# Decays kept on the chip, one transfer for r and the values, in a chunked recurrence with a mixture of experts behind it

## The chip, the cores and the metric

The kernel runs on one core of one Trainium2 chip. A core has TensorE (PE; PEld is its weight load), VectorE (DVE), ScalarE (ACT), GpSimd (POOL) and SyncE (SP), which here does nothing but issue transfers to the DMA engines. The metric is device time of one execution in microseconds (us).

## The reference: a recurrence, then a mixture of experts

For 4 sequences, 8 heads, 768 tokens and 40 dimensions a head, a 40 x 40 state is carried from token to token:

```python
for t in range(S):
    y[:, :, t] = np.einsum('bhd,bhde->bhe', rt, state)
    Sa = np.einsum('bhde,bhe->bhd', state, at)
    state_decay = state * wt[:, :, None, :] - np.einsum('bhd,bhe->bhde', Sa, bt)
    state = state_decay + np.einsum('bhd,bhe->bhde', vt, kt)
```

The 3072 x 320 outputs go through 8 experts of width 1024 (two products with a ReLU between). Each token's 8 outputs are weighted with a matrix P, made from a gate's logits by eight rounds of row and column normalisation over all tokens, and added up.

## The kernel before, in words

The sequence is cut into 12 chunks of 64 tokens. A unit of work is one chunk of one sequence, its 8 heads as 4 pairs: 48 units, numbered 4 x chunk + sequence. Each unit has three stages.

*Preparation* (`prep`). SP loads one tile of inputs (inp: decays, k, b, a). DVE makes the decays' running products with two scans (q, L124, and g, L134). POOL or DVE scales k and b (kb, L147) and a (ab, L153 and L154), PE forms the products ll (L159) and transposes kb (kt, L167), DVE masks ll into sx (L169), ACT copies the rest. What the recurrence needs later is kept in one of NSX sets (sx, bb, cc), used in turn: unit n + NSX writes where unit n lay. The running products g themselves are not in a set: they are stored to memory outside the chip (gd, L138) and loaded again (gl, L278) when the unit's output is scaled.

*Inverse*. Two chunks together (8 units) need triangular inverses. The factors are stored (ld), loaded in another layout (lu, L380), inverted in about 40 DVE instructions (L184 to L207), stored (ud, nd, L371 and L372) and loaded again by `tload` as operands for PE (lg, td and tt, L243 to L252); `tmat` makes the last blocks (gp and op, L261 and L266).

*Recurrence* (`recur`), five steps a unit, the four sequences interleaved: av (L289) from the values and the state (vz) and r (rb); f (L290); xc (L297); x and c copies on ACT; pu (L308) with the inverse; pm (L310); c (L315); ws (L317) on DVE; then POOL makes y = ws x decays (L321) and the next state z (L330), which PE transposes (zt) and ACT copies into the next vz.

A list of events with due times gives all this an order in the program, and a planner of the compiler, with a timing model of its own, sets each engine's final order. Every engine works through its instructions strictly in that order, SP too: a transfer that must wait holds up all transfers behind it on SP.

The mixture of experts follows in the same program. Its tiles take the place of the tiles of the attention stage, and its first weights are loaded and cast while the last recurrences run.

Of the kernel before, what the change touches and what calls it, by code (L numbers as in the profile page):

```python
# [11 lines left out]
F32 = mybir.dt.float32  # L12
# [6 lines left out]
C = 64  # L19
NCH = S // C  # L20
# [9 lines left out]
def attention(ctx, tc, d, xd, ps, pq, pt, gs, lg):  # L30
# [5 lines left out]
    io = ctx.enter_context(tc.tile_pool(name="a_io", bufs=1))  # L36
# [12 lines left out]
    sx_b, bb_b, cc_b = ([None] * NSX for _ in range(3))  # L49
    raws = {}  # L50
    for n in range(NCH * NB - NSX, NCH * NB):
        i, pool = n % NSX, sets[n - NCH * NB + NSX]
        if i in IN_SETS or i in KB_SETS:
            raw = pool.tile([128, 1252], F32, name=f"st{i}")
            raws[i] = raw
            sx_b[i] = raw[0:R2, 0:832].rearrange("r (p h x) -> r p h x", h=2, x=104)
            bb_b[i] = raw[:, 832:1248].rearrange("r (p x) -> r p x", x=104)
            cc_b[i] = raw[0:R2, 1248:1252]
            continue
        sx_b[i] = pool.tile([R2, NP, 2, 104], F32, name=f"sx{i}")  # L60
# [26 lines left out]
    def clear():  # L87
# [3 lines left out]
        for t in vz_b + rb_b + c1_b + lg_b:  # L91
            nc.vector.memset(t, 0.0)
# [13 lines left out]
    state = {"sx": 0, "ab": 0, "g1": 0, "vz": 0, "c1": 0, "t1": 0, "tt": 0, "rb": 0, "y": 0}  # L106
# [8 lines left out]
    def prep(c, b, ld):  # L115
# [15 lines left out]
        bb, cc = bb_b[i], cc_b[i]  # L131
        ge = pin.tile([RL, NP, 65], F32, name="g", bufs=2)
# [4 lines left out]
        gd = dr.tile([RL, 320], F32, name=f"gd{cb}", bufs=1)  # L137
        nc.sync.dma_start(out=gd[:, 0:260], in_=ge.rearrange("r p t -> r (p t)"))  # L138
# [40 lines left out]
        return dict(cc=cc, g=gd, sx=sx, bb=bb)  # L179
# [53 lines left out]
    def tload(c):  # L233
# [6 lines left out]
        u = [[slice(cc * 64 + blk * 32 + h * 16, cc * 64 + blk * 32 + h * 16 + 16) for h in range(2)]  # L240
             for blk in range(2)]
# [3 lines left out]
        for h in range(2):  # L245
            nc.sync.dma_start(out=t1[q[h]], in_=nd[u[0][h]].rearrange("g j s -> j g s"))
# [23 lines left out]
    def recur(c, b):  # L270
        pp = preps[c, b]
        vz, zc = vz_cur[b], zp[b]
        nc.sync.dma_start(out=vz[:, :, 0:64], in_=d["v"][c, b])
        rb = rot("rb", rb_b)
        for h in range(2):
            nc.sync.dma_start(out=rb[h * 64:h * 64 + 48, :, h * 64:h * 64 + 64], in_=d["r"][c, b, h])
        gl = io.tile([RL, NP, 65], F32, name="gl", bufs=2)
        nc.sync.dma_start(out=gl.rearrange("r p t -> r (p t)"), in_=pp["g"][:, 0:260])  # L278
# [9 lines left out]
        for p in range(NP):  # L288
            nc.tensor.matmul(av[:, p], lhsT=vz[0:R2, p], rhs=rb[0:R2, p], start=True, stop=True)  # L289
# [31 lines left out]
        nc.gpsimd.tensor_tensor(out=y[0:R2, :, b % 2], in0=ws[:, :, 0:64], in1=gl[0:R2, :, 0:64], op=ALU.mult)  # L321
# [14 lines left out]
        vz = rot("vz", vz_b)  # L336
        nc.scalar.copy(out=vz[0:40, :, 64:104], in_=zt[:, :, 0:40])
        nc.scalar.copy(out=vz[64:104, :, 64:104], in_=zt[:, :, 64:104])
        zp[b] = z
        vz_cur[b] = vz  # L340
# [20 lines left out]
    vz_cur = [rot("vz", vz_b) for _ in range(NB)]  # L361
# [12 lines left out]
    def load_lu(s, n):  # L374
        ld = invs[s][0]
        for cc in range(n):
            for blk in range(2):
                for h in range(2):
                    u0, r0 = cc * 64 + blk * 32 + h * 16, blk * 32
                    nc.sync.dma_start(  # L380
                        out=lu[u0:u0 + 16],
# [454 lines left out]
```

## Time and profile before

| | us |
|---|---|
| median of 3 runs | 1839.33 (1838.09 to 1847.54) |
| the profiled execution | 1832.94 |
| its span, first to last instruction | 1831.2 |
| DMA busy share, 125 to 375 us | 0.79 |

A row of the page or of an answer names the engine, the line, the operation and the tiles (out<-in), then how often it ran, its busy time in us and the mean ns of one, then the engine's idle time before it and what ended that idle time. A wait row reads: who waited, for whom, total us, number of waits, longest. In rows of issues, SPq is SP's queue, and the ns are those of issuing, not of the transfer's landing.

### The profile page before, as it was taken

To read this page: it belongs to the slowest core of one execution; us is meant where nothing else is said; L and a number is where in the kernel's file an instruction comes from. 1 tells how busy PE (TensorE), PEld (TensorE's weight loads), DVE (VectorE), ACT (ScalarE), POOL (GpSimd) and SP (SyncE) were. 2 spreads that over 40 slices of the span, in tenths; PEclk is the share of its full clock that TensorE was granted. 3 is DMA by queue.
4 is the path that set the end of the run, shared out by engine and by line. 5 is a ranking of instruction groups with operands and counts; after the bars stand their busy time and mean duration, and the time that the engine had idled before them with its cause. 6 is when DMAs were issued, how large, how long until landed. Compare 5 with 4: busy or idle time off the path is not lost.

```text
span 1831.2 us, 31655 instructions
## 1 busy us (share of the span) xinstructions
PE 1724.3 (94%) x11843; PEld 1696.8 (93%) x11843; DVE 1365.3 (75%) x2356; ACT 856.8 (47%) x1851; POOL 874.0 (48%) x854
## 2 busy tenths in 40 slices
PE   4479988999989999999999999999999999999999
PEld 4368888898978999999999999999999999999999
DVE  7786996973788867777676878977686877767675
ACT  6347767766743533434343434345343343424342
POOL 6545664723462626447291735008182644628160
PEclk8568988999999999999999999999999999999999
DMA  7468777867520101111020112201020111102001
GB/s 193 116 157 185 175 180 174 186 137 172 152 77 20 57 20 57 38 39 57 20 75 20 57 37 61 69 1 60 16 76 20 57 38 38 57 20 75 15 24 44
DMA packets 211759, 140.47 MB, mean 77 GB/s; under 512 B 162965, under 2 KB 193813, under 8 KB 211605
## 3 DMA queue, kind: packets, MB, share of 16 engines
q1 hardware_dynamic: 207925, 132.70, 27.9%
q10 hardware_dynamic: 3680, 5.74, 1.2%
q8 instruction: 94, 1.54, 0.3%
q14 instruction: 60, 0.49, 0.1%
HBM read 110.78 MB, written 27.61 MB: 76 GB/s over the span
## 4 chain that ended last, share of the span: by engine, by line
PE 75%; DVE 7%; DMA 4%; issue 4%; POOL 3%; ACT 2%; SPq 2%; POOLq 0%; ACTq 0%; DVEq 0%
PE op L647 36%; PE p L582 33%; DMA inp<-in_inp_dram 1%; PE xc L297 1%; PE av L289 1%; PE pu L308 1%; DVE pr L193 1%; DVE hl L606 1%; DVE q L124 1%; PE c L315 1%; DMA ld<-lt 1%; PE op L266 1%; DVE sm L600 1%; PE ll L159 1%; POOL ab L154 1%
## 5 line engine op out<-in xcount | busy, mean ns | idle before, releaser
L582 PE MATMUL p<-xch,wh 128*128 128x384 f32 (+1 forms) x1792 | 605.0, 339 | 8.9 <-DVE sm L600 4.3
L603 ACT ACTIVATE hh<-sm 128x384 fp32r<-128x384 f32 x512 | 269.5, 527 | 728.5 <-DVE sm L600 728.4
L647 PE MATMUL op<-wh,hh 128*128 128x320 f32 x1536 | 477.2, 311 | 4.0 <-ACT hh L603 3.8
L647 PE MATMUL op<-wl,hh 128*128 128x320 f32 x1536 | 474.8, 310 | 0.0
L647 PE MATMUL op<-wh,hl 128*128 128x320 f32 x1536 | 468.0, 309 | 0.9 <-DVE hl L606 0.9
L528 POOL TENSOR_TENSOR wl<-ws,wh 128x640 fp32r<-128x640 f32 x60 | 103.1, 1718 | 606.2 <-ACT wh L526 606.1
L606 DVE SCALAR_TENSOR_TENSOR hl<-sm,hh 128x384 fp32r<-128x384 f32 x512 | 373.1, 762 | 2.6 <-ACT hh L603 1.8
L582 PEld LDWEIGHTS p<-xch,wh 128*128 128x128 f32 (+1 forms) x1792 | 337.0, 188 | 13.3 <-DVE sm L600 5.2
L582 PE MATMUL p<-xcl,wh 128*128 128x384 f32 x896 | 302.3, 337 | 0.0
L582 PE MATMUL p<-xch,wl 128*128 128x384 f32 x896 | 301.8, 337 | 0.0
L647 PEld LDWEIGHTS op<-wh,hh 128*128 128x128 f32 x1536 | 290.2, 189 | 4.9 <-ACT hh L603 4.9
L647 PEld LDWEIGHTS op<-wl,hh 128*128 128x128 f32 x1536 | 291.1, 190 | 0.0
L647 PEld LDWEIGHTS op<-wh,hl 128*128 128x128 f32 x1536 | 286.8, 188 | 1.4 <-DVE hl L606 1.2
L600 DVE TENSOR_TENSOR sm<-p,u 128x384 f32<-128x384 f32 x384 | 236.3, 625 | 8.7
L582 PEld LDWEIGHTS p<-xcl,wh 128*128 128x128 f32 x896 | 168.6, 188 | 0.0
L582 PEld LDWEIGHTS p<-xch,wl 128*128 128x128 f32 x896 | 168.5, 188 | 0.0
L600 DVE TENSOR_TENSOR sm<-p,p 128x384 f32<-128x384 f32 x128 | 71.3, 557 | 129.4 <-PE p L582 75.0
L600 DVE TENSOR_TENSOR p<-p,p 128x384 f32<-128x384 f32 x128 | 71.1, 556 | 101.7 <-PE p L582 101.4
L600 DVE TENSOR_TENSOR u<-p,p 128x384 f32<-128x384 f32 x128 | 70.8, 553 | 57.1 <-PE p L582 55.9
L536 POOL TENSOR_TENSOR wl<-ss,wh 128x512 fp32r<-128x512 f32 x60 | 90.3, 1505 | 28.4 <-ACT wh L533 24.2
L159 PE MATMUL ll<-ab,kb 104*128 104x128 f32 x336 | 62.8, 344 | 40.5 <-POOL kb L147 18.5
L159 PEld LDWEIGHTS ll<-ab,kb 104*128 104x128 f32 x336 | 54.2, 244 | 45.3 <-POOL kb L147 24.8
(163 smaller groups left out, 2727.3 us busy)
## 6 DMA issues: line engine op xcount, KB each, us to landing
ws<-in_wts_dram SPq DMA_DIRECT2D x60, 832.0 KB, 4.5
inp<-in_inp_dram SPq DMA_DIRECT2D x42, 451.5 KB, 4.5
gd<-g SPq DMA_DIRECT2D x48, 113.8 KB, 2.6
gl<-gd SPq DMA_DIRECT2D x48, 113.8 KB, 2.8
vz<-in_v_dram SPq DMA_DIRECT2D x48, 112.0 KB, 3.5
xd<-y SPq DMA_DIRECT2D x24, 224.0 KB, 3.5
ld<-lt ACTq DMA_DIRECT2D x40, 128.0 KB, 2.6
rb<-in_r_dram SPq DMA_DIRECT2D x96, 48.0 KB, 3.1
```

Source lines behind the costliest of these rows:

```text
L124: nc.vector.tensor_tensor_scan(out=qr.rearrange("r p t -> r (p t)"), data0=w65[:, 260:0:-1], data1=one65, initial=0.0, op0=ALU.mult, op1=A ...
L154: eng.tensor_tensor(out=ab[64:104, :, 64:128], in0=a_in[64:104], in1=g[64:104], op=ALU.mult)
L159: nc.tensor.matmul(ll[:, p], lhsT=kb[:, p], rhs=ab[:, p], start=True, stop=True)
L193: nc.vector.tensor_tensor(out=prv, in0=a.unsqueeze(2).broadcast_to([nu, n_c, n_r, n_k]), in1=m.unsqueeze(1).broadcast_to([nu, n_c, n_r, n_ ...
L266: nc.tensor.matmul(op[:, p], lhsT=gs[:, p], rhs=t2[:, p], start=True, stop=True)
L528: g.tensor_tensor(out=wl[:, 0:640], in0=raw[:, 256:896], in1=wh[:, 0:640], op=ALU.subtract)
L536: g.tensor_tensor(out=lv[:, 3:7], in0=so[:, :, 0], in1=hv[:, 3:7, 0], op=ALU.subtract)
L582: nc.tensor.matmul(o, lhsT=w_, rhs=x_, start=(j == 0), stop=(j == 3))
L600: eng.tensor_tensor(out=out, in0=x, in1=y, op=ALU.add)
L603: nc.scalar.activation(out=hh[:, f, h], in_=sm[f][:, h], func=AF.Relu)
L606: v.scalar_tensor_tensor(out=hl[:, f, h], in0=sm[f][:, h], scalar=0.0, in1=hh[:, f, h], op0=ALU.max, op1=ALU.subtract)
L647: nc.tensor.matmul(ops[i], lhsT=a[:, h, cs], rhs=w_[:, cw], start=(f == 0 and h == 0 and j == 0), stop=(last and h == 1 and j == 2))
```

## The change

The running products g stay on the chip: each set gets a fourth part (ge), into which the scan writes and from which y is scaled. The store gd and the load gl are gone. A set is larger by that, and there are 19 instead of 23. The values and r, r already with its zero blocks, lie side by side in one array and come in one transfer into a tile rv of 5 buffers, which also holds the transposed state; before, the values came in one transfer and r in two, one for each head of a pair, r into 2 buffers that had been cleared once. In the inverse's layout the two heads of a pair now alternate instead of lying in two blocks, so that one load brings both: lu takes 2 loads a chunk instead of 4, the operands td 2 instead of 4. Three small constant tiles (pmat, ones, ident) move behind the weights' tiles. In the arithmetic nothing changes.

```diff
-    sx_b, bb_b, cc_b = ([None] * NSX for _ in range(3))
+    sx_b, bb_b, cc_b, ge_b = ([None] * NSX for _ in range(4))
...
-            raw = pool.tile([128, 1252], F32, name=f"st{i}")
+            raw = pool.tile([128, 1512], F32, name=f"st{i}")
...
+            ge_b[i] = raw[0:RL, 1252:1512].rearrange("r (p t) -> r p t", t=65)
...
+        ge_b[i] = pool.tile([RL, NP, 65], F32, name=f"ge{i}")
...
-    vz_b = [const.tile([RL, NP, 104], F32, name=f"vz{i}") for i in range(5)]
+    rv_b = [const.tile([RL, NP, 232], F32, name=f"rv{i}") for i in range(5)]
     c1_b = [const.tile([R2, NP, 104], F32, name=f"c1{i}") for i in range(2)]
-    rb_b = [const.tile([RL, NP, 128], F32, name=f"rb{i}") for i in range(NRB)]
...
-        for t in vz_b + rb_b + c1_b + lg_b:
+        for t in [x[:, :, 192:232] for x in rv_b] + c1_b + lg_b:
             nc.vector.memset(t, 0.0)
...
-        bb, cc = bb_b[i], cc_b[i]
-        ge = pin.tile([RL, NP, 65], F32, name="g", bufs=2)
+        bb, cc, ge = bb_b[i], cc_b[i], ge_b[i]
         g = ge[:, :, 0:64]
...
-        gd = dr.tile([RL, 320], F32, name=f"gd{cb}", bufs=1)
-        nc.sync.dma_start(out=gd[:, 0:260], in_=ge.rearrange("r p t -> r (p t)"))
...
-        return dict(cc=cc, g=gd, sx=sx, bb=bb)
+        return dict(cc=cc, g=g, sx=sx, bb=bb)
...
-        u = [[slice(cc * 64 + blk * 32 + h * 16, cc * 64 + blk * 32 + h * 16 + 16) for h in range(2)]
-             for blk in range(2)]
+        un_, nn_ = ([t[cc * 64 + blk * 32:cc * 64 + blk * 32 + 32].rearrange("(g h) j s -> (h j) g s", h=2)
+                     for blk in range(2)] for t in (ud, nd))
...
-        for h in range(2):
-            nc.sync.dma_start(out=t1[q[h]], in_=nd[u[0][h]].rearrange("g j s -> j g s"))
-        for h in range(2):
-            nc.sync.dma_start(out=t2[q[h]], in_=ud[u[1][h]].rearrange("g j s -> j g s"))
+        nc.sync.dma_start(out=t1, in_=nn_[0])
+        nc.sync.dma_start(out=t2, in_=un_[1])
...
-                nc.sync.dma_start(out=tt[r, :, r], in_=ud[u[blk][h]].rearrange("g j s -> j g s"))
+                nc.sync.dma_start(out=tt[r, :, r], in_=un_[blk][h * 32:h * 32 + 32])
...
-        vz, zc = vz_cur[b], zp[b]
-        nc.sync.dma_start(out=vz[:, :, 0:64], in_=d["v"][c, b])
-        rb = rot("rb", rb_b)
-        for h in range(2):
-            nc.sync.dma_start(out=rb[h * 64:h * 64 + 48, :, h * 64:h * 64 + 64], in_=d["r"][c, b, h])
-        gl = io.tile([RL, NP, 65], F32, name="gl", bufs=2)
-        nc.sync.dma_start(out=gl.rearrange("r p t -> r (p t)"), in_=pp["g"][:, 0:260])
+        rv, zc = rv_cur[b], zp[b]
+        nc.sync.dma_start(out=rv[:, :, 0:192], in_=d["rv"][c, b])
...
-            nc.tensor.matmul(av[:, p], lhsT=vz[0:R2, p], rhs=rb[0:R2, p], start=True, stop=True)
+            nc.tensor.matmul(av[:, p], lhsT=rv[0:R2, p, 128:232], rhs=rv[0:R2, p, 0:128], start=True, stop=True)
...
-        nc.gpsimd.tensor_tensor(out=y[0:R2, :, b % 2], in0=ws[:, :, 0:64], in1=gl[0:R2, :, 0:64], op=ALU.mult)
+        nc.gpsimd.tensor_tensor(out=y[0:R2, :, b % 2], in0=ws[:, :, 0:64], in1=pp["g"][0:R2], op=ALU.mult)
...
-        vz = rot("vz", vz_b)
-        nc.scalar.copy(out=vz[0:40, :, 64:104], in_=zt[:, :, 0:40])
-        nc.scalar.copy(out=vz[64:104, :, 64:104], in_=zt[:, :, 64:104])
+        rv = rot("rv", rv_b)
+        nc.scalar.copy(out=rv[0:40, :, 192:232], in_=zt[:, :, 0:40])
+        nc.scalar.copy(out=rv[64:104, :, 192:232], in_=zt[:, :, 64:104])
...
-                for h in range(2):
-                    u0, r0 = cc * 64 + blk * 32 + h * 16, blk * 32
-                    nc.sync.dma_start(
-                        out=lu[u0:u0 + 16],
-                        in_=ld[cc, r0:r0 + 32].rearrange("j b p h s -> (b p) j h s")[:, :, h, r0:r0 + 32])
+                u0, r0 = cc * 64 + blk * 32, blk * 32
+                nc.sync.dma_start(out=lu[u0:u0 + 32],
+                                  in_=ld[cc, r0:r0 + 32].rearrange("j b p h s -> (b p h) j s")[:, :, r0:r0 + 32])
...
-NSX = 23
+NSX = 19
...
-    pmat = one.tile([128, 24, E], F32, name="pmat")
     lg = one.tile([128, 24, E], F32, name="lg")
-    ones = one.tile([128, 128], F32, name="ones")
-    ident = one.tile([128, 128], F32, name="ident")
...
+    two = ctx.enter_context(tc.tile_pool(name="two", bufs=1))
+    pmat = two.tile([128, 24, E], F32, name="pmat")
+    ones = two.tile([128, 128], F32, name="ones")
+    ident = two.tile([128, 128], F32, name="ident")
...
-    rb = np.zeros((NCH, NB, 2, 48, NP, C), np.float32)
-    rb[:, :, :, 0:40] = split(g["r"])
+    rb = np.zeros((NCH, NB, RL, NP, 2 * C), np.float32)
+    x = split(g["r"])
+    rb[:, :, 0:40, :, 0:C], rb[:, :, 64:104, :, C:] = x[:, :, 0], x[:, :, 1]
...
-    arrays = dict(inp=inp, r=rb, v=packed(g["v"]),
-                  vt=vt, wts=wts, gate=gate, cst=cst)
+    arrays = dict(inp=inp, rv=np.concatenate([rb, packed(g["v"])], -1), vt=vt, wts=wts, gate=gate, cst=cst)
```

What the lines don't show is how the planner orders the engines anew. Two places follow, each first before and then with the change; rows are an engine's instructions in the order of its queue (line, operation, out<-in, shape, "x2" for two alike in a row). The first is SP's queue at the end of the second inverse, where operands of chunk 2 are loaded and the input tiles of later preparations with them. Before:

```order
L276 DMA rb_232<-in_r_dram 48x4x64
L371 DMA ud<-un 64x1024 x2
L372 DMA nd<-tn 64x1024 x2
L278 DMA gl<-gd_431 112x260
L324 DMA xd<-y_234 448x1x128
L138 DMA gd_1468<-g 112x260
L118 DMA inp<-in_inp_dram 112x1032
L276 DMA rb_232<-in_r_dram 48x4x64
L118 DMA inp<-in_inp_dram 112x1032
L243 DMA lg<-ld 32x16x32 x2
L246 DMA td<-nd 32x16x32 x2
```

With the change:

```order
L270 DMA f<-in_vt_dram 64x8x40
L268 DMA rv_205<-in_rv_dram 112x4x192
L361 DMA ud<-un 64x1024
L362 DMA nd<-tn 64x1024
L361 DMA ud<-un 64x1024
L362 DMA nd<-tn 64x1024
L314 DMA xd<-y_213 448x1x128
L118 DMA inp<-in_inp_dram 112x1032
L240 DMA lg<-ld 32x16x32 x2
L242 DMA td<-nd 64x16x32
L118 DMA inp<-in_inp_dram 112x1032
L243 DMA td<-ud 64x16x32
```

The gl, gd and rb transfers between the inverse's stores and the loads of inp are gone, the two td<-nd are one; the values' and r's load is the one row rv.

The second place is DVE around the ws of recurrence 3 (the fourth unit), its first row in both. In brackets stands what the instruction waits for: PE, Activation, Pool and DVE are engines, DMAHW a transfer. Before:

```order
L317 TENSOR_TENSOR ws<-c_1450,c_230 104x416 [waits PE_49,Activation_49]
L128 RECIPROCAL g_223<-q 112x4 [waits DVE_49]
L134 SCALAR_TENSOR_TENSOR g<-inp,g_223 112x260 [waits DMAHW5_49,DVE_49]
L310 TENSOR_TENSOR pm<-pu,cst 128x416 [waits PE_49]
L169 TENSOR_TENSOR sx_205<-ll,cst 64x8x64 [waits PE_49]
L290 TENSOR_TENSOR f<-av,cst 104x8x64 [waits PE_49]
L124 SCALAR_TENSOR_TENSOR q<-inp,cst 112x260 [waits DMAHW7_49,Pool_49]
L169 TENSOR_TENSOR sx_208<-ll,cst 64x8x64 [waits PE_49]
L128 RECIPROCAL g_223<-q 112x4 [waits DVE_49]
L134 SCALAR_TENSOR_TENSOR g<-inp,g_223 112x260 [waits DMAHW4_49,DVE_49]
L317 TENSOR_TENSOR ws<-c_1652,c_229 104x416 [waits PE_49,Activation_49]
```

With the change (ge_176 is the decays' place in the set that unit 3 used and that unit 22 takes over):

```order
L307 TENSOR_TENSOR ws<-c_1319,c_211 104x416 [waits PE_49,Activation_49]
L166 TENSOR_TENSOR sx_169<-ll,cst 64x8x64 [waits PE_49]
L133 SCALAR_TENSOR_TENSOR ge_176<-inp,g_204 112x260 [waits Pool_49]
L300 TENSOR_TENSOR pm<-pu,cst 128x416 [waits PE_49]
L280 TENSOR_TENSOR f<-av,cst 104x8x64 [waits PE_49]
L124 SCALAR_TENSOR_TENSOR q<-inp,cst 112x260 [waits DMAHW5_49,Pool_49]
L128 RECIPROCAL g_204<-q 112x4 [waits DVE_49]
L166 TENSOR_TENSOR sx_173<-ll,cst 64x8x64 [waits PE_49]
L307 TENSOR_TENSOR ws<-c_1428,c_210 104x416 [waits PE_49,Activation_49]
L300 TENSOR_TENSOR pm<-pu,cst 128x416 [waits PE_49]
L124 SCALAR_TENSOR_TENSOR q<-inp,cst 112x260 [waits DMAHW2_49,DVE_49,Pool_49]
L133 SCALAR_TENSOR_TENSOR ge_180<-inp,g_204 112x260 [waits Pool_49]
```

The scan of a preparation (L134 before, L133 now) waited for the store of an earlier scan's result; it now waits for POOL, whose y reads the old decays, and it stands two rows behind the ws that y needs. Of the 29 scans of units 19 to 47 all wait for POOL, and from 1 to 6 instructions lie between ws and scan.

More of the change, by code (lines that the diff above doesn't have):

```diff
@@ L35, in attention @@
     const = ctx.enter_context(tc.tile_pool(name="a_const", bufs=1))
-    io = ctx.enter_context(tc.tile_pool(name="a_io", bufs=1))
     wk = ctx.enter_context(tc.tile_pool(name="a_wk", bufs=2))
@@ L104, in first_use @@
                            in_=cst[64:R2, 360:400].unsqueeze(1).broadcast_to([40, 8, 40]))
-    state = {"sx": 0, "ab": 0, "g1": 0, "vz": 0, "c1": 0, "t1": 0, "tt": 0, "rb": 0, "y": 0}
+    state = {"sx": 0, "ab": 0, "g1": 0, "rv": 0, "c1": 0, "t1": 0, "tt": 0, "y": 0}
     def rot(key, lst):
@@ L335, in recur @@
             nc.tensor.transpose(zt[:, p], z[:, p], ident[0:R2, 0:R2])
-        vz = rot("vz", vz_b)
-        nc.scalar.copy(out=vz[0:40, :, 64:104], in_=zt[:, :, 0:40])
-        nc.scalar.copy(out=vz[64:104, :, 64:104], in_=zt[:, :, 64:104])
+        rv = rot("rv", rv_b)
+        nc.scalar.copy(out=rv[0:40, :, 192:232], in_=zt[:, :, 0:40])
+        nc.scalar.copy(out=rv[64:104, :, 192:232], in_=zt[:, :, 64:104])
         zp[b] = z
-        vz_cur[b] = vz
+        rv_cur[b] = rv
     def gate(c, b, y):
@@ L360, in attention @@
     ys = {}
-    vz_cur = [rot("vz", vz_b) for _ in range(NB)]
+    rv_cur = [rot("rv", rv_b) for _ in range(NB)]
     preps, invs, tts = {}, {}, {}
@@ L431 @@
 SKEW = 1.1
-NSX = 23
+NSX = 19
 GL = 3
 NFB = 3
-NRB = 2
 KB_POOL = (1,2,3,4,5,6,7)
@@ L483, in body @@
         attention(actx, tc, d, xd, ps, pq, pt, gs, lg)
-        nc.gpsimd.memset(ones, 1.0)
-        nc.sync.dma_start(out=ident, in_=d["cst"][:, 232:360])
     stg = ctx.enter_context(tc.tile_pool(name="stg", bufs=2))
@@ L490, in body @@
     x1 = ctx.enter_context(tc.tile_pool(name="x1", bufs=1))
+    two = ctx.enter_context(tc.tile_pool(name="two", bufs=1))
+    pmat = two.tile([128, 24, E], F32, name="pmat")
+    ones = two.tile([128, 128], F32, name="ones")
+    ident = two.tile([128, 128], F32, name="ident")
+    nc.gpsimd.memset(ones, 1.0)
+    nc.sync.dma_start(out=ident, in_=d["cst"][:, 232:360])
     po = ctx.enter_context(tc.tile_pool(name="po", bufs=1, space=bass.MemoryType.PSUM))
```

## The prediction

> **What bounds the kernel now.** I read the page first, then the table of stretches, then the chain and the waits of the stretch that the change touches most.
>
> ```profile
> span 1831.2 us, 31655 instructions
> PEclk8568988999999999999999999999999999999999
> 0.00:125.00 125.00, 65.24 (x347) 58.56 (x348) 94.71 (x171) 58.18 (x145) 73.58 (x105) 0.63 0.65 155
> 125.00:375.00 250.00, 225.99 (x2115) 216.83 (x2113) 201.33 (x343) 180.14 (x455) 145.23 (x170) 0.92 0.79 179
> 375.00:505.00 130.00, 124.42 (x1202) 118.78 (x1201) 80.37 (x149) 84.71 (x202) 44.77 (x54) 0.96 0.65 150
> 550.00:1831.00 1281.00, 1272.65 (x7985) 1269.19 (x7984) 950.90 (x1639) 516.24 (x1019) 580.77 (x500) 1.00 0.13 42
> ```
>
> The last four rows are stretches of the span: length, busy time of PE, PEld, DVE, ACT and POOL, granted clock, DMA share, GB/s. From 550 us on, PE is busy 1272.65 of 1281 us at full clock. That is the mixture of experts, which the change leaves alone, so nothing is to be had there. Everything is decided in the first 505 us: a prologue (to 125) in which DVE is the busiest engine, the recurrence with preparations in between (125 to 375), and the recurrence alone (375 to 505), where PE is busy 96%. In the middle stretch PE is busy 226 and DVE 201 of 250 us, neither full, and the clock is 0.92. Something else ends waits there:
>
> ```profile
> by line: issue 17.0%; DMA inp<-in_inp_dram 10.3%; DVE pr L193 4.6%; PE ll L159 4.1%; POOL ab L154 3.5%; DVE q L124 3.4%; DVE gt L196 3.3%; POOL y L321 3.1%; PE av L289 3.1%; DMA lu<-ld 2.9%; PE xc L297 2.6%; POOL z L330 2.5%; PE op L266 2.4
> DVE q L124 <- DMA inp<-in_inp_dram: 16.6, 8, 5.6
> PE av L289 <- DVE ws L317: 6.6, 3, 3.1
> 152.07 1.61 SPq L372 DMA_DIRECT2D nd<-tn  x2
> 153.78 1.29 SPq L278 DMA_DIRECT2D gl<-gd  x1
> 155.12 0.61 SPq L324 DMA_DIRECT2D xd<-y  x1
> 155.83 0.57 SPq L138 DMA_DIRECT2D gd<-g  x1
> 156.45 0.46 SPq L118 DMA_DIRECT2D inp<-in_inp_dram  x1
> 156.96 0.64 SPq L276 DMA_DIRECT2D rb<-in_r_dram  x1
> 157.70 0.54 SPq L118 DMA_DIRECT2D inp<-in_inp_dram  x1
> 162.46 0.70 DVE L124 TENSOR_TENSOR_SCAN q<-inp,cst 112x260 f32<-112x260 f32 x1 [5.08 <-DMA inp<-in_inp_dram]
> ```
>
> The first row is the chain by line within 125 to 375 us. The largest named item is the load of a preparation's inputs: 10.3% of 250 us, 26 us. DVE waits for it 16.6 us in 8 waits. The timeline under it shows one: SyncE (SP) issues back to back from 152 us on, the load that DVE needs comes last, at 157.70, and DVE stands still 5.08 us until 162.46. So SP's issuing is the resource that is short.
>
> **The change, part by part.** SP's issue cost in this stretch, count and min/median/max ns of an issue:
>
> ```profile
> L276 SPq DMA_DIRECT2D rb<-in_r_dram x56: 564/594/1277, 125.9 to 374.1; - x56
> L273 SPq DMA_DIRECT2D vz<-in_v_dram x25: 572/602/1493, 128.4 to 371.8; - x25
> L278 SPq DMA_DIRECT2D gl<-gd x27: 303/430/1358, 131.0 to 368.4; - x27
> L138 SPq DMA_DIRECT2D gd<-g x29: 304/430/1346, 124.8 to 367.3; - x29
> L380 SPq DMA_DIRECT2D lu<-ld x29: 303/484/1532, 144.6 to 374.8; - x29
> L246 SPq DMA_DIRECT2D td<-nd x12: 420/598/1057, 160.0 to 353.3; - x12
> SPq L278 <- POOL y L321: 12.5, 9, 2.7
> SPq L138 <- DVE g L134: 10.6, 12, 1.7
> ```
>
> *Issues removed.* By medians: r 56 x 0.594 = 33.3 us, values 25 x 0.602 = 15.1, decays back 27 x 0.430 = 11.6, decays out 29 x 0.430 = 12.5, half of the lu loads 14.5 x 0.484 = 7.0, half of the td loads (12 of nd, about as many of ud, at 0.598 at most) 12 x 0.598 = 7.2. Sum 86.7. Added: 28 loads of rv; none exists in the trace. It writes 448 rows, as the values' load did, so I take 0.602, sum 16.9; if it cost the largest issue seen, 1.493, it would be 41.8. Net 70 us (45 at worst) of 250 us of SP's time. The two waits in the last rows, 23 us, go too: SP no longer stands behind a scan (L134) or the multiplication of y (L321) for a store or load of decays.
>
> *What that is worth.* SP's time is not the path; the late input load is. Its wait of 16.6 us is bounded below by 0 (if the buffer, not SP, made it late) and above by 16.6. The timeline above shows SP busy ahead of the load, so I take 10. The PE idles that follow such a wait also lower the clock: 0.92 of 250 us is 20 us of rate lost, from which I take 4, bounds 0 and 20.
>
> [...]
>
> *Bytes.*
>
> ```profile
> gd<-g SPq DMA_DIRECT2D x29, 113.8 KB, 2.8
> gl<-gd SPq DMA_DIRECT2D x27, 113.8 KB, 3.0
> vz<-in_v_dram SPq DMA_DIRECT2D x25, 112.0 KB, 3.8
> rb<-in_r_dram SPq DMA_DIRECT2D x56, 48.0 KB, 3.4
> nd<-tn SPq DMA_DIRECT2D x8, 256.0 KB, 4.7
> td<-nd SPq DMA_DIRECT2D x12, 64.0 KB, 4.1
> ```
>
> A recurrence moved 112 + 2 x 48 + 2 x 113.8 = 436 KB; now 112 rows x 4 x 192 values x 4 B = 336 KB, zeros included. The DMA share of 0.79 falls rather than rises, and I give this no term of its own. That av now needs one large transfer instead of three is hidden by how early it is issued: five buffers instead of r's two.
>
> *Prologue.* There, too, SP stood behind scans and POOL behind stores that SP had yet to issue:
>
> ```profile
> SPq L138 <- DVE g L134: 22.8, 12, 4.7
> POOL st L102 <- DMA ld<-st: 3.3, 3, 2.4
> ```
>
> I take 3.3 us for POOL, about 2 for four fewer lu and td issues (4 x 0.5) between the first inverse and its matrices, and leave the clearing of the smaller tiles out. Sum 5, bounds -2 (the first inverse is now interleaved with another preparation) and 10.
>
> *19 sets instead of 23: a new wait.* The decays now lie in the set, and POOL's y of recurrence n reads them. The scan of preparation n + 19 overwrites them, so each of the 29 scans from number 19 on waits for POOL; the order puts it 2 to 7 DVE instructions behind the ws of that same recurrence. Behind the scan on DVE stand pm, f and the inverse, and PE waits for those.
>
> ```profile
> L321 POOL TENSOR_TENSOR y<-ws,gl 104x256 f32<-104x256 f32 x28 | 23.6, 842 | 29.9 <-DVE ws L317 27.2 <-issue 1.7 <-DVE g L128 0.2
> L147 POOL TENSOR_TENSOR kb<-inp,q 104x512 f32<-104x512 f32 x29 | 36.5, 1259 | 34.1 <-DVE q L124 19.5 <-PE kt L167 7.1 <-PE xc L297 6.1
> L169 DVE TENSOR_TENSOR sx<-ll,cst 64x512 f32<-64x512 f32 x22 | 14.8, 671 | 5.0 <-PE ll L159 4.9
> L310 DVE TENSOR_TENSOR pm<-pu,cst 128x416 f32<-128x416 f32 x28 | 16.0, 572 | 2.8 <-PE pu L308 2.8
> ```
>
> If y starts as soon as ws is done it takes 0.84 us; sx and pm between ws and the scan cover 0.67 to 1.24 us, and the wait is near 0. If one kb stands ahead of y on POOL it is 1.26 + 0.84 - 0.67 = 1.4 us, and 29 x 1.4 = 41. POOL's y mostly waited for DVE (27.2 of its 29.9 idle us), so the first case is the common one; I take 0.17 us each, 5 in all, bounds 0 and 41.
>
> A second price of the 19 sets: preparations 24 to 47 come later, and the last inverse ends one to two recurrences nearer to its use. From its end to the first matrix lie the store of nd (4.7) and the load of td (4.1), some 9 us. Between 375 and 505 us 20 recurrences take 130 us, 6.5 each, so 1.5 of them are about 10 us: just covered, and 0 is taken; uncovered it is up to 4 us for each of three inverses.
>
> *End of the attention stage.* In the stretch from 375 to 505 us ScalarE stood behind the first weights' load, with the copy that PE needs queued behind it:
>
> ```profile
> 446.23 0.83 ACT L522 CAST wh<-ws 128x768 fp32r<-128x768 f32 x1 [3.68 <-DMA xd<-y]
> 448.35 1.12 PE L289 MATMUL av<-rb,vz 104*104 104x128 f32 x8 [1.78 <-ACT vz L338]
> ```
>
> In the new order the cast comes one recurrence later behind the same load. I take back the 1.8 us of PE and 1 of clock, 3 in all (bounds 0 and 8). Moving the three constant tiles behind the weights costs nothing: the transpose that reads ident comes well after the recurrence's end, and the mixture's order on PE is unchanged from there.
>
> *Sum.* 5 + 10 + 4 + 3 - 5 = 17 us less. The profiled execution took 1832.94 us (span 1831.2), so it would take 1816. The median of the runs is 1839.33, 6.4 above it; I take the same 17 from that: **1822 us**.
>
> **The rivals.** *The clock comes back, PE becomes the bound.* If SP was behind most of what stands still, all of 16.6 and most of the 20 us of rate return with the prologue's 5: 37 less, 1802. For it speaks that 375 to 505, without preparations, already runs at 96% PE; against it that DVE's 201 of 250 us leave little below 225 for that stretch.
>
> [...]
>
> *The load was late for another reason.* Input tiles have two buffers, and the load waits for POOL's kb and ab of two preparations before. If that ends last, DVE's 16.6 us stay, and the change is 1839 less 5 plus 5: 1839. For it speaks that POOL waits for q in turn (19.5 us above), a loop that SP is not in; against it the timeline.
>
> *The scan behind y decides; slower.* From 17/29 = 0.6 us more per scan on, the gain is gone. At 1 us each it is 29 less the other terms' 22, so 7 more, 1846; at 1.4 it is 41 - 22 = 19 more, 1858. Typical 1851. For it speaks that nearly every scan is set to follow the recurrence that frees its set; against it DVE's 49 idle us, which take part of it.
>
> **How the numbers follow.** The forecast 0.48 (own range 1808 to 1832), clock 0.13, other reason 0.22, scan 0.17. The range 1796 to 1848 leaves out about 0.06 below and 0.13 above. About 0.5%, 9.2 us, is what a measurement can tell, so 1830 to 1848.5 is the same: faster 0.45 of the forecast's 0.48 and the clock's 0.13, 0.58; slower 0.16 of the scan's 0.17; the same 0.26.
>
> **What would show it.** Right: DVE's waits for inp in the middle stretch fall below 8 us, that stretch ends sooner, and DVE's scans wait for POOL under 6 us in all. The clock rival: a clock above 0.97 there. The other reason: inp is issued right behind POOL's ab, and waited for as before. The scan: a large row of DVE waiting for POOL y. I am wrong at the root if the first 505 us do not shrink though SP issues with gaps.

## The result, and the profile after

Beside the kernel before on the same chip, the changed kernel took 1822.54 us (median of 4, 1817.39 to 1826.81) against 1840.9 (4 runs): ratio 0.9894, 95% interval 0.9856 to 0.9932. The same comparison a second time, with 7 and 26 runs, gave 1827.64 against 1838.0, ratio 0.9943, interval 0.9919 to 0.9967. The gain is thus real; the two measurements put it at 18 and at 10 us. One execution of all that follow, of the kernel with one-row transfers, was slow at 3357 us and is counted nowhere. The two profiled executions stand 9.8 us apart (1832.94 and 1823.17), and what follows is about those 9.8.

The page and the table of stretches of the changed kernel, in the columns of the prediction's first fence:

```profile
span 1821.3 us, 31276 instructions
PEclk7568999998899999999999999999999999999999
DMA packets 178730, 135.51 MB, mean 74 GB/s; under 512 B 119189, under 2 KB 160789, under 8 KB 178581
0.00:125.00 125.00, 65.94 (x363) 59.52 (x364) 97.94 (x173) 60.44 (x150) 69.37 (x100) 0.63 0.64 152
125.00:375.00 250.00, 235.25 (x2253) 225.07 (x2252) 197.92 (x348) 187.07 (x473) 139.78 (x173) 0.95 0.77 172
375.00:505.00 130.00, 123.69 (x1102) 117.68 (x1100) 84.42 (x147) 79.17 (x184) 47.90 (x54) 0.91 0.56 130
550.00:1821.00 1271.00, 1263.28 (x7931) 1260.41 (x7929) 941.71 (x1622) 512.00 (x1008) 581.28 (x500) 1.00 0.13 42
```

From 125 to 375 us PE is busy 9.3 us longer than before in the same time, and the clock is 0.95 instead of 0.92. From 375 to 505 us it is the other way: 0.91 instead of 0.96. To compare like with like, I cut both traces where ws (DVE) of units 0, 21, 39 and 47 ends. First the kernel before, then the changed one; the columns are the same.

```profile
130.10:325.20 195.10, 176.65 (x1613) 169.53 (x1611) 155.41 (x274) 137.83 (x349) 110.27 (x132) 0.90 0.79 178
325.20:453.90 128.70, 119.82 (x1207) 113.95 (x1206) 86.76 (x147) 87.72 (x220) 54.33 (x65) 0.98 0.74 164
453.90:504.30 50.40, 49.82 (x463) 48.18 (x462) 33.92 (x66) 35.14 (x80) 24.39 (x27) 0.94 0.57 147
```

```profile
128.90:300.60 171.70, 162.27 (x1540) 155.18 (x1539) 137.86 (x242) 129.49 (x327) 101.83 (x124) 0.94 0.79 176
300.60:430.90 130.30, 125.06 (x1256) 119.72 (x1254) 97.59 (x175) 91.82 (x233) 48.55 (x64) 0.97 0.74 164
430.90:495.10 64.20, 59.32 (x468) 56.38 (x466) 37.98 (x67) 38.24 (x85) 32.30 (x34) 0.81 0.49 120
```

Length less PE's busy time is PE's idle time: before 18.5, 8.9 and 0.6 us, 27.9 in all; after 9.4, 5.2 and 4.9, 19.5 in all. PE's busy time over the three is the same, 346.3 and 346.7 us. So what the profiled pair gained between units 0 and 47, 8.0 us, is idle time of PE and nothing else, and 1.2 us more came in the prologue (unit 0 ends at 128.9 instead of 130.1). The clock gave 9 us and took 9: the rate lost (1 less the clock, times the length) fell from 19.5 to 10.3 us in the first row and rose from 3.0 to 12.2 in the last. Up to unit 21 the changed kernel was 24.6 us ahead; at unit 47 it was 9.2 ahead, and the mixture kept that. The lead at unit 21 is in part work put off: with 19 sets fewer preparations are done by then. PE has 73 records fewer up to there (1540 and 1613) and 49 more up to unit 39 (1256 and 1207). At unit 39, where all preparations are done in both, the lead is 23.0 us.

Now the waits that the prediction spoke of, from 125 to 375 us of the changed kernel (who waits, for whom, us, times, longest), and two rows of SP's issues there (ns min/median/max). The third row, with L154, is of the kernel before.

```profile
DVE q L124 <- DMA inp<-in_inp_dram: 25.6, 11, 5.0
DVE st L133 <- POOL y L311: 0.4, 1, 0.4
SPq L118 <- POOL ab L154: 4.6, 4, 2.4
SPq L118 <- POOL ab L151: 9.6, 9, 1.9
SPq L314 <- POOL z L320: 28.7, 8, 4.9
SPq L270 <- PE xc L287: 17.1, 11, 6.0
L268 SPq DMA_DIRECT2D rv<-in_rv_dram x28: 573/585/3245, 130.6 to 357.4; - x28
L118 SPq DMA_DIRECT2D inp<-in_inp_dram x27: 318/338/1993, 133.2 to 352.3; - x27
```

SP now stands waiting for work to become ready (28.7 us for z and 17.1 for xc; 144 us in all its waits, before 67): its time is not short. Yet DVE waits for its inputs longer than before, 25.6 us instead of 16.6, and SP stands longer at the load of inp until POOL's ab has freed the buffer, 9.6 us instead of 4.6. The new wait of the scans for POOL's y is 0.4 us.

### The profile page after: what moved, and what is told of

Same layout as the page of the kernel before. It is cut to its first block, busy times and chain, and to the rows that moved or that the text cites. A ratio compares the mean times of both kernels' runs of the same rounds, so it can differ in the third digit from the quotient of the medians.

```text
span 1821.3 us, 31276 instructions
## 1 busy us (share of the span) xinstructions
PE 1724.8 (95%) x11843; PEld 1697.1 (93%) x11843; DVE 1362.4 (75%) x2354; ACT 855.4 (47%) x1847; POOL 863.8 (47%) x850
## 4 chain that ended last, share of the span: by engine, by line
PE 77%; DVE 3%; DMA 2%; ACT 1%; issue 1%; POOL 1%; SPq 0%; DVEq 0%; ACTq 0%; POOLq 0%
PE op L635 36%; PE p L570 34%; PE xc L287 1%; PE pu L298 1%; PE c L305 1%; PE av L279 1%; PE gp L256 1%; DVE hl L594 1%; DVE sm L588 1%; PE op L261 1%; DMA nd<-tn 0%; PE zt L325 0%; PE ll L156 0%; PE lp L335 0%; DMA ws<-in_wts_dram 0%
## 5 line engine op out<-in xcount | busy, mean ns | idle before, releaser
L699 DVE SCALAR_TENSOR_TENSOR acc<-op,pmat,acc 128x320 f32<-128x320 f32 x168 | 91.3, 543 | 4.5 <-PE op L635 4.4
```

The costliest lines, as they stand in the source:

```text
L699: nc.vector.scalar_tensor_tensor(out=acc[:, m], in0=ops[i], scalar=pmat[:, n, e:e + 1], in1=acc[:, m], op0=ALU.mult, op1=ALU.add)
```

## The experiments

There were twelve more measurements: the changed kernel again, and eleven others. Each is given with the median of its runs and its ratio to the kernel before on its chip. Every run also has a mean granted clock of PE over the span, and within one kernel the times follow it, most clearly where it varies most: the 12 runs of the kernel with 19 sets and decays on the chip go from 1817.05 us at 0.961 to 1838.87 at 0.950. A common slope fitted through all 194 runs, with a level for each kernel, is 1.28 us for each 0.001 of clock, and leaves a spread of 2.6 us where the kernels' own is 4.4. The last column but one is a kernel's level less that of the kernel before at a common clock (95% within about 2 us, 2.7 for the kernels with 4 runs). It is a second reading and no replacement of the ratio, since a part of the clock may belong to a kernel: the mean over the runs is 0.9549 for the kernel before and 0.9590 for the changed one.

| kernel | median us | ratio, interval | at a common clock | MB moved |
|---|---|---|---|---|
| the change, first time | 1822.5 | 0.9894 (0.9856 to 0.9932) | -7.2 | 135.5 |
| the change again | 1827.6 | 0.9943 (0.9919 to 0.9967) | -5.0 | 135.5 |
| 19 sets alone | 1840.2 | 1.0029 (1.0010 to 1.0048) | +2.7 | 140.5 |
| 19 sets, decays | 1823.3 | 0.9945 (0.9919 to 0.9971) | -8.1 | 129.3 |
| 19 sets, decays, r with v (no heads) | 1833.1 | 0.9986 (0.9960 to 1.0011) | -4.4 | 135.5 |
| 19 sets, decays, heads (no r with v) | 1826.1 | 0.9926 (0.9901 to 0.9951) | -8.8 | 129.3 |
| heads alone | 1823.9 | 0.9944 (0.9923 to 0.9965) | -5.7 | 140.5 |
| change + unused transfers | 1837.9 | 1.0010 (0.9984 to 1.0037) | +2.8 | 146.7 |
| change + one-row transfers | 1820.3 | 0.9914 (0.9897 to 0.9931) | -8.1 | 135.6 |
| no r with v, zeros beside v | 1819.8 | 0.9912 (0.9896 to 0.9927) | -9.7 | 134.8 |
| no r with v, 20 sets | 1832.4 | 0.9999 (0.9977 to 1.0021) | -1.0 | 129.3 |
| no r with v, 3 input buffers | 1820.2 | 0.9911 (0.9895 to 0.9927) | -12.5 | 129.3 |
| change, first casts on POOL | 1840.6 | 1.0020 (1.0004 to 1.0036) | +5.3 | 135.5 |

One thing holds for all: the compiler's planner gives each of these kernels an order of its own. Compared in ten pairs by the order of the rows in the traces, 10 to 16% of the DVE rows stand elsewhere, and 22 to 53% of SP's. No experiment changes one thing alone.

### The parts, one after another

The first theory (A) was the prediction's: SP's queue made shorter is the gain. The rivals were the order that fewer sets give (B), their shorter lead (C), and the wait for the decays' round trip (D).

19 sets alone:

```diff
-NSX = 23
+NSX = 19
```

> The kernel before with 19 preparation sets instead of 23, nothing else: the decays still go to DRAM and back, r and v still come in three transfers, and SP issues as many DMAs as before. Theory A (the gain is SP's queue made shorter): no gain, 1841 us within 4, and the end of unit 21 stays at 325 us within 4. Theory B (the gain is the order that fewer sets give, with the preparations spread over later units): most of the 18 us are here, 1823 to 1830 us, and unit 21 ends near 305 us. Theory C (fewer sets cost, since the preparations have less lead): 1845 us or more.

0.3% slower, not faster. B falls: fewer sets are a price, as C had it, of 3 to 5 us, though the middle went faster in its profile too (unit 21 ended at 307.7 us, near B's 305).

With the decays kept on the chip on top of that:

```diff
+        bb, cc, ge = bb_b[i], cc_b[i], ge_b[i]
...
-        nc.sync.dma_start(out=gd[:, 0:260], in_=ge.rearrange("r p t -> r (p t)"))
...
-        nc.sync.dma_start(out=gl.rearrange("r p t -> r (p t)"), in_=pp["g"][:, 0:260])
```

> The kernel before with 19 sets and the decays kept on the chip: the store of the decays (48) and their load (48) are gone, two of SP's issues per unit, some 0.55 us each, while r and v still come in three transfers and the inverse still loads by head. Theory A: somewhat under half of the net 70 us of issues that the whole change takes off SP in the middle stretch, so 7 to 9 us faster than with 19 sets alone (about 1832 us), unit 21 near 315 us. Theory B: no more than 2 us between this run and the one with 19 sets alone. Theory D (the DRAM round trip itself was what was waited for, not the queue): all of the gain is here, about 1823 us.

17 us faster than 19 sets alone (11 at a common clock), both measured beside the same runs of the kernel before. All of the change's gain is here, more than A's 7 to 9 and as D had it.

The changed kernel without the heads' part, that is, the last kernel with r and v joined (the three constant tiles, pmat, ones and ident, move with it; shown is a part of the edit against the changed kernel):

```diff
-        nc.sync.dma_start(out=t1, in_=nn_[0])
-        nc.sync.dma_start(out=t2, in_=un_[1])
+        for h in range(2):
+            nc.sync.dma_start(out=t1[q[h]], in_=nd[u[0][h]].rearrange("g j s -> j g s"))
+        for h in range(2):
+            nc.sync.dma_start(out=t2[q[h]], in_=ud[u[1][h]].rearrange("g j s -> j g s"))
```

> The changed kernel with the inverse's layout put back (its loads and stores by head, 2 more DMAs in each tload and 2 more in each load of lu per chunk): the rest is the change. Theory A: 2 to 4 us slower than the changed kernel, 1825 to 1827 us. Theory B: within 2 us of the changed kernel if the order of the preparations is kept, about 1823 us. Theory D: 1823 us too. Were it the one DMA with alternating heads that costs (narrower rows), this run is the faster one, under 1820 us.

The joined transfer takes two issues a unit off SP, and the kernel is 10 us slower than the one without it (4 at a common clock). A had promised the opposite. The means of the two are 7.8 us apart, and the 4.2 of them beyond the common clock are the clock: it was 0.9536 on average over these 12 runs, 0.9569 over the other's.

The heads alone, on the kernel before (the first lines of the edit):

```diff
-        u = [[slice(cc * 64 + blk * 32 + h * 16, cc * 64 + blk * 32 + h * 16 + 16) for h in range(2)]
-             for blk in range(2)]
+        un_, nn_ = ([t[cc * 64 + blk * 32:cc * 64 + blk * 32 + 32].rearrange("(g h) j s -> (h j) g s", h=2)
+                     for blk in range(2)] for t in (ud, nd))
```

> The kernel before with the heads alternating in the inverse, and nothing else: 23 sets, the decays by DRAM, r and v apart. Theory A: 2 to 4 us faster than before, about 1838 us. Theories B and D: within 2 us of before, 1841 us.

10 us faster by itself (6 at a common clock), more than any theory gave it. This part takes some 48 issues off SP and no bytes (140.5 MB as before), in the kernel before, whose SP had less slack (its waits from 125 to 375 us add up to 67 us, in the changed kernel to 144), so it speaks for A there as far as 6 us speak. On top of 19 sets and decays (the kernel without r with v, below) the same edit gave 0.2% by ratio, 0.9945 to 0.9926, which is within the error.

The changed kernel again, and the changed kernel with r and v apart as before (and the three constant tiles where they were):

> The changed kernel once more, in the company of the kernels it is compared with (its first measurement had 4 runs). Its first ratio to the kernel before, 0.989, would put it near 1815 us where the kernel before takes 1834 us. The single parts gave +5 us (19 sets), -11 (19 sets and decays), -1 (those and r with v) and -10 (heads alone) against the kernel before. If the parts add, the changed kernel is the run without heads less the 10 us of the heads alone: 1822 to 1824 us. If 1815 us holds, heads are worth more together with the rest than alone.

```diff
-        nc.sync.dma_start(out=rv[:, :, 0:192], in_=d["rv"][c, b])
+        nc.sync.dma_start(out=vz[:, :, 0:64], in_=d["v"][c, b])
+        for h in range(2):
+            nc.sync.dma_start(out=rb[h * 64:h * 64 + 48, :, h * 64:h * 64 + 64], in_=d["r"][c, b, h])
```

> The changed kernel without the joined transfer: 19 sets, decays on the chip and heads alternating, but r (two transfers) and v (one) apart as before. Theory A (SP's queue made shorter is what counts): it issues two DMAs a unit more than the changed kernel, so it is 5 to 9 us slower, 1822 us or more where the changed kernel takes 1815. Theory E (the joined transfer costs, as the run with 19 sets and decays against that with r and v joined too says, +10 us): it is the faster of the two, 1813 us or less. If the +10 us was the clock alone, which was at half rate for 31 and 37.5 us at the end of those two attentions in their profiles, both are within 4 us of each other.

By the medians the parts add, as the expectation for the changed kernel had it: 1827.6 us is 10 under before. At a common clock they don't: 4.4 without the heads and 5.7 for the heads alone would be 10.1, and the changed kernel is 5.0 under. The kernel without the joined transfer, measured beside it, is 1.6 us from it, so within the 4 us that the expectation left to the clock. It is no slower, though SP issues two DMAs a unit more: A fails here for the second time.

### Issues, bytes or the wait

The decays' transfers put back into the changed kernel, with no engine using what they bring:

```diff
+        nc.sync.dma_start(out=gd[:, 0:260], in_=ge.rearrange("r p t -> r (p t)"))
...
+        gl = wk.tile([RL, NP, 65], F32, name="gl", bufs=1)
+        nc.sync.dma_start(out=gl.rearrange("r p t -> r (p t)"), in_=pp["gd"][:, 0:260])
```

> The changed kernel with the decays' store and load put back as transfers whose result is not used: SP issues 96 DMAs more (some 0.55 us each), and nobody waits for them. Theory A: SP's queue is what counts, so about half of the gain is lost, 7 to 9 us slower than the changed kernel. Theory D (the wait for the decays' round trip was what counted): no difference, within 3 us of it. Theory B (order by the sets): no difference either, unless the order of the preparations moves.

The whole gain is gone, 10 us (8 at a common clock). So it was not POOL's wait for the decays to come back (D); SP still waits for these transfers, which the rows below show. Issues or what they carry are left, and the next kernel parts them: the same 96 transfers, with one row of each.

```diff
-        nc.sync.dma_start(out=gd[:, 0:260], in_=ge.rearrange("r p t -> r (p t)"))
+        nc.sync.dma_start(out=gd[0:1, 0:260], in_=ge[0:1].rearrange("r p t -> r (p t)"))
...
-        nc.sync.dma_start(out=gl.rearrange("r p t -> r (p t)"), in_=pp["gd"][:, 0:260])
+        nc.sync.dma_start(out=gl[0:1].rearrange("r p t -> r (p t)"), in_=pp["gd"][0:1, 0:260])
```

> As the run with the decays' transfers put back unused, but each carries one row of 260 numbers in place of 104: SP issues the same 96 DMAs more than the changed kernel, with a hundredth of the bytes. Over the eight kernels so far the time at a common clock follows the bytes moved (129.3 MB: 9 us under before; 135.5 MB: 5 to 7 under; 140.5 MB with 19 sets: 2 over; 146.7 MB: 3 over) and not SP's issue time from 125 to 375 us (160 us in the fastest, 145 us in the slowest of those with the decays on the chip). Theory F (bytes on the 16 DMA engines in the attention): within 2 us of the changed kernel, some 6 us under before. Theory A (issues): as the run with the whole transfers, 2 us over before or thereabouts.

Nothing is lost. The two kernels differ by 1% in ratio and by 11 us at a common clock, with intervals far apart. Rows of both: bytes, the stretch from 125 to 375 us (columns as above), DVE's waits for lu from 125 to 425 us, SP's waits at gl in the same time and the issue of gl. First the whole transfers, then one row each.

```profile
DMA packets 191019, 146.71 MB, mean 80 GB/s; under 512 B 120725, under 2 KB 173077, under 8 KB 190869
125.00:375.00 250.00, 230.87 (x2156) 219.92 (x2156) 195.22 (x343) 180.49 (x456) 146.97 (x173) 0.93 0.84 193
DVE lu L199 <- DMA lu<-ld: 14.8, 4, 6.9
SPq L272 <- DMA gl<-gd: 11.5, 4, 4.3
SPq L272 <- DMA gd<-ge: 8.9, 10, 2.4
L272 SPq DMA_DIRECT2D gl<-gd x28: 303/314/2382, 129.6 to 370.6; - x28
```

```profile
DMA packets 178924, 135.64 MB, mean 75 GB/s; under 512 B 119285, under 2 KB 160981, under 8 KB 178773
125.00:375.00 250.00, 234.38 (x2288) 223.12 (x2287) 201.19 (x357) 190.57 (x481) 150.48 (x176) 0.97 0.80 177
DVE lu L199 <- DMA lu<-ld: 3.1, 2, 2.6
SPq L272 <- DMA gl<-gd: 13.1, 5, 3.0
SPq L272 <- DMA gd<-ge: 5.6, 6, 2.4
L272 SPq DMA_DIRECT2D gl<-gd x29: 215/288/1897, 128.3 to 370.8; - x29
```

The issue takes SP about as long in both (314 and 288 ns), and SP waits at gl for the transfers ahead of it about as long too (20.4 us and 18.7 in the two rows), so neither of these parts the two kernels. With the whole transfers the DMA engines are busier (0.84 against 0.80), and the inverse's load lu, which stands in no relation to the decays, is waited for 14.8 us instead of 3.1. That wait is not shown to be the price, though: the kernel before waited 6.1 us for lu and 19 sets alone 0.9, both with the whole transfers.

So 96 issues more cost nothing in the changed kernel, where SP has slack, with the reservation that the two kernels have different orders. What issues cost in the kernel before, where SP had less, no run shows; the heads alone are the nearest to it.

Is it then any byte? The kernel with r and v apart, each load of v with as many zeros beside the values, in the same number of rows (198,700 packets in both; how the tile and the array grow is not shown):

```diff
-        nc.sync.dma_start(out=vz[:, :, 0:64], in_=d["v"][c, b])
+        nc.sync.dma_start(out=vz[:, :, 0:128], in_=d["v"][c, b])
...
-            nc.tensor.matmul(av[:, p], lhsT=vz[0:R2, p], rhs=rb[0:R2, p], start=True, stop=True)
+            nc.tensor.matmul(av[:, p], lhsT=vz[0:R2, p, 64:168], rhs=rb[0:R2, p], start=True, stop=True)
```

> The changed kernel without the joined transfer (the fastest so far), where each load of v carries as many zeros beside the values: the same issues, the same rows, 5.1 MB more, and nobody reads the zeros. Theory F: 3 to 5 us slower than without the zeros, so 4 to 6 us under before at a common clock, as the changed kernel is, whose joined transfer brings 5.5 MB of zeros. Theory A: no difference, 9 us under before.

5.5 MB more, and no slower (9.7 us under before against 8.8, at a common clock). So theory F, that each MB has its price, falls in this form. The decays moved twice that, half of it as writes to memory outside the chip, each followed by a read of the same bytes. They also add packets, 12,095 between the two kernels above, where the zeros add none; but the joined transfer takes some 20,000 away (198,700 to 178,731) and gained nothing. Which of these counts, the amount, the writes, the packets or where the planner then puts the other loads, stays open.

### Two sizes

The room that r and v apart leave was used for a 20th set, and in another kernel for a third buffer of the inputs:

```diff
-NSX = 19
+NSX = 20
```

> The changed kernel without the joined transfer, and the room that this leaves used for a 20th set. If a lead of one more unit is worth something (the run with 19 sets alone was 2 us over before at a common clock, so four sets cost 2 us at most): within 2 us of the same kernel with 19 sets, some 9 us under before. If the order that the planner makes of it decides, it may be 5 us to either side.

```diff
-        inp = raws[IN_MAP[cb]][0:RL, 0:1032] if IN_MAP.get(cb) else pin.tile([RL, 1032], F32, name="inp", bufs=2)
+        inp = raws[IN_MAP[cb]][0:RL, 0:1032] if IN_MAP.get(cb) else pin.tile([RL, 1032], F32, name="inp", bufs=3)
```

> The changed kernel without the joined transfer, and the room that this leaves used for a third buffer of the input's tile. If the two buffers are why the preparations stand late behind their input (DVE waits 16 us in 8 for it from 125 to 440 us there, and the loads are issued within a few us of the buffer's release): these waits fall under 5 us and the attention ends 5 to 10 us sooner, 14 to 19 us under before. If the preparations are not on the path that sets the end: the waits fall and the time stays within 3 us of 9 under before. If the loads only start sooner and share the same DMA engines: the waits stay.

One set more made it 8 us slower at a common clock (13 by ratio), where more lead should not hurt. So another order of the same work can be worth some 8 us, and no part above can be priced more closely than that. The decays' transfers are hardly above it, 8, 11 and 11 us at a common clock in three pairs of kernels; what speaks for them is that all three pairs came out the same way.

The third buffer, the wait it was made for (125 to 440 us), and the stretches between units 0, 21, 28, 39 and 47:

```profile
DVE q L125 <- DMA inp<-in_inp_dram: 8.3, 2, 6.0
124.90:289.80 164.90, 158.25 (x1556) 151.45 (x1556) 143.84 (x243) 129.73 (x327) 103.76 (x124) 0.97 0.75 165
289.80:354.80 65.00, 59.58 (x533) 57.04 (x532) 50.84 (x93) 45.34 (x115) 36.31 (x42) 0.88 0.68 144
354.80:431.30 76.50, 76.26 (x728) 73.46 (x727) 47.52 (x85) 47.40 (x121) 15.43 (x22) 0.90 0.53 114
431.30:492.10 60.80, 55.96 (x468) 53.80 (x466) 38.33 (x66) 38.04 (x83) 31.74 (x34) 0.86 0.52 145
```

With two buffers these waits were 16.3 us in 8, and the same four stretches took 176.0, 58.8, 69.5 and 59.5 us at clocks of 0.94, 1.00, 1.00 and 0.86. So the two buffers account for about half of the late load's waits, and units 0 to 21 took 11 us less with three. The next two stretches, at lower clocks, gave 13 back. The ratio, 0.9911, is not told apart from the 0.9926 with two buffers; at a common clock it is 4 us better.

### What gave the gain back at the end

In the changed kernel's last units ACT stood behind inputs of the mixture (timeline; in brackets the idle time before, and what ended it), and DVE behind the first x (425 to 475 us):

```profile
431.95 0.83 ACT L510 CAST wh<-ws 128x768 fp32r<-128x768 f32 x1 [2.68 <-DMA ws<-in_wts_dram]
442.28 0.83 ACT L544 CAST xch<-xs 128x768 fp32r<-128x768 f32 x1 [2.01 <-DMA xs<-xd]
445.74 0.83 ACT L544 CAST xch<-xs 128x768 fp32r<-128x768 f32 x1 [2.10 <-DMA xs<-xd]
471.04 0.62 ACT L549 CAST xch<-xt 128x512 fp32r<-128x512 f32 x1 [3.38 <-DVE xt L546]
DVE xt L542 <- DMA xs<-xd: 5.7, 1, 5.7
```

So these casts and differences were moved to POOL (three of the eight changed lines are shown):

```diff
-        nc.scalar.copy(out=wh[:, 640:1408], in_=raw[:, 896:1664])
+        cast(k < 2, wh[:, 640:1408], raw[:, 896:1664])
...
-        g = nc.gpsimd if s == 1 else v
+        g = nc.gpsimd if s < 2 else v
...
-        nc.scalar.copy(out=xh[:, 0:3, :, cu], in_=bv)
+        cast(s == 0, xh[:, 0:3, :, cu], bv)
```

Here `cast` is a copy on POOL where its first argument holds, on ACT otherwise; the other casts of the two blocks and of x are treated alike.

> The changed kernel with the first two weight blocks and the first segment's three blocks of x (the mixture's first inputs) cast on POOL in place of ACT, and their differences on POOL in place of DVE, nothing else: in the changed kernel's trace ACT stood 2.7, 2.0, 2.1 and 3.4 us and DVE 5.7 us behind late inputs of these between 430 and 471 us, while units 39 to 47 took 64 us instead of 50. If these waits are what gave 13 us of the gain back: 5 to 13 us faster than the changed kernel and units 39 to 47 in 50 to 57 us. If the half-rate clock there (20.5 us of it, against 10.2 before) is the cause and not the effect: within 3 us of it, with units 39 to 47 at 60 us or more. If POOL becomes late with y or with the first blocks: slower, with the mixture's first product waiting on POOL.

Of this kernel: units 39 to 47, the same stretch for the mixture's first products alone (PE and PEld), PE's waits from 486 to 560 us, and one row of its timeline.

```profile
431.30:486.60 55.30, 45.81 (x441) 44.08 (x439) 22.47 (x40) 24.43 (x60) 32.26 (x40) 0.91 0.43 105
431.30:486.60 55.30, 1.29 (x6) 1.00 (x6) 0.91 0.43 105
PE p L576 <- POOL xch L497: 15.9, 1, 15.9
PE p L576 <- DVE xcl L562: 5.4, 1, 5.4
449.76 0.39 PE L256 MATMUL gp<-td,lg 64*64 64x32 f32 x2 [6.45 <-DMA td<-nd]
```

The units take 55 us, as the first expectation had it, but for another reason: the changed kernel has 32 of the mixture's products among them (8.3 us of PE), this one 6. Without the products it is 54 against 56 us. The waits went, and one of 6.45 us for a load of the inverse came in their place; then PE stood 15.9 us for POOL's last casts, and the kernel is 13 us slower than the change. So it is not shown that the casts in ACT's way gave the 13 us back, nor is it excluded, since new waits came with moving them. What is left in that stretch of the changed kernel is 4.3 us of idle time and 9.2 of clock, and the cause of the clock is not settled.

The longer end goes with the sets. In the profiles, units 39 to 47 take 50.4 and 51.8 us in the two kernels with 23 sets (before, and heads alone), 59.7 with 20, and 55 to 66 in the eleven profiles with 19. Of these, 19 sets alone, where nothing else is changed, takes 60.1 us (445.8 to 505.9) with PE busy 49.9 us of it at a clock of 0.84; it was 8 us ahead of the kernel before at unit 39 and 2 behind at unit 47. So 9.7 of the 13.8 us given back at the end come with the 19 sets alone; by which order or wait, one profile of each kernel does not show.

None of the eleven others is shown to beat the changed kernel: the best three, at 0.991 with intervals up to 0.993, overlap with both intervals that the change itself got.

## Why the prediction came out right

The time was right (1822 forecast, 1822.5 and 1827.6 measured), the reasons mostly were not, and so luck had a part in it. The 17 us were met by the first comparison alone (18 us); the second and the profiled pair have 10, and the common clock 5 to 7. Point by point:

- *What bounds.* That only the first 505 us count held: from the mixture's first layer-2 product on (505.3 us before, 496.2 now) all is shifted by 9 us, and less than 1 us comes behind it. What the pair gained there between units 0 and 47 is idle time of PE (27.9 to 19.5 us).
- *Issues, 70 us off SP: the step that failed.* SP's time was sized well (rv was put at 0.602 us an issue and took 0.585); what failed is the step from it to the gain. Read from one stretch of the timeline, it was that the late load came from SP's back-to-back issues; but over that whole stretch SP had waited 67 of 250 us. With SP relieved, DVE waited for the load longer; 96 issues put back into the changed kernel cost nothing; the joined transfer, which saved issues, gained nothing. What the decays' part took away that counted was the transfers themselves, as far as three pairs with different orders show it. I had given the bytes "no term", having seen that they fall.
- *The late load, -10.* DVE's wait for inp rose from 16.6 to 25.6 us, so the criterion I had named (below 8) was missed, while the units did end sooner, 24.6 us at unit 21 and 23.0 at unit 39. A wait on DVE was no measure of the path, and neither is unit 21: 19 sets alone reached it 17.5 us sooner than before and ended later. The rival "late for another reason" had named its sign, inp issued behind POOL's ab and waited for as before, and that is what the rows show (9.6 us instead of 4.6); the third buffer took away half of the wait. As a time, 1839, it was wrong.
- *The clock, -4.* Over the profiled pair the rate lost is 25.1 and 26.4 us, so nothing. Over the runs the changed kernel's clock is 0.9590 against 0.9549 before, which by the slope is 5 us. The size was about right by the runs; in the profile the end took back what the first units gained. That a lower clock follows such a wait the trace of the kernel before shows for the one in the prediction: behind it PE stood 2.97 us for ws until 165.63, and the clock was 0.50 from 166.1 to 172.9. The length of a wait does not tell it: one of 0.80 us until 186.42 was followed by 0.50 (186.6 to 193.4), one of 2.08 us until 437.18 by 1.00 (to 446.4). The 4 was my estimate.
- *Prologue, -5.* 1.2 us.
- *End of the attention, -3.* Wrong sign: units 39 to 47 took 64.2 us instead of 50.4, 4.3 of it idle and 9.2 clock. I had followed one cast; four waits of ACT, 10 us, now lay there, and 19 sets alone already had 60.1 us.
- *The scan behind y, +5.* 0.4 us in the changed kernel. POOL had been waiting for ws itself in 31 of the 48 units and did y at once. The slower rival, with 0.17, found no support here.
- *19 sets, 0.* Four sets fewer cost 3 to 5 us by themselves, and with them came the longer end.

In the profiled pair the terms thus came to 9 us up to unit 47 instead of 17, wrong in both directions: 22 us instead of 14 from unit 0 to unit 39, with 0 lost instead of 5 for the scan, 13 to 14 lost instead of 3 gained at the end, and 1 gained instead of 5 at the start.

## What to carry to other kernels

When a queue looks full, put the issues back with next to no bytes before believing that issuing is the price; here two kernels told more than any row of the trace. Try it where the queue is full, too; here it was done only where SP had slack. Where a planner reorders the whole program at every edit, run a neutral edit or two (one buffer, one set) to learn how much another order is worth, and don't price parts below that. Record the mean clock with each run: it accounted for about two thirds of the variance within the kernels. Compare two traces only at points by which the same work is done.

## What was not expected of the hardware

In one of these runs PE's clock stayed at half rate for 37.5 us while PE was busy without a pause, and got there with no pause longer than 1.7 us in the 13.8 us ahead of it. This is the kernel with r and v joined but without the heads' part, before, in and after that stretch:

```profile
425.00:438.80 13.80, 12.10 (x132) 11.80 (x130) 8.04 (x15) 8.61 (x23) 2.32 (x3) 1.00 0.69 150
438.80:476.30 37.50, 37.50 (x214) 36.02 (x213) 11.76 (x21) 19.11 (x43) 12.53 (x14) 0.50 0.72 188
476.30:500.00 23.70, 22.03 (x219) 20.50 (x219) 20.78 (x31) 16.97 (x38) 17.52 (x18) 1.00 0.39 110
```

PE is busy 37.50 of 37.50 us at 0.50, and a busy row takes 175 ns on average (37.50/214) against 92 ahead of it (12.10/132), so the half rate is real. In the 13.8 us before, PE was idle for 1.7 us in all; its longest wait from 400 to 515 us is 1.7, for a load of the inverse (td). The half-rate stretches between units 0 and 47 lasted 3.4, 6.8, 10.2 and 20.5 us in the kernel before and the changed one, and late ones of 30.7 and 37.5 us stand in two others (19 sets with the decays, and those with r and v joined). Nor did shorter waits bring the clock back, as the prediction's rival had it: the kernel with three input buffers had clocks of 0.88 and 0.90 after unit 21 (289.8 to 354.8 and 354.8 to 431.3 us), where two buffers had 1.00, and that behind its fastest units, at 0.97. What starts and ends these stretches, the runs do not show.
